# Spreading feed-forward filler and weight rounding over the turns of an attention loop

## The chip, the core and the metric

The kernel runs on one core of a Trainium2 chip. The metric is the device time of one execution in microseconds (us). Engines are named as in the profile: PE is TensorE, with PEld its weight loads; DVE is VectorE, ACT ScalarE, POOL GpSimd, SP the queue that issues most transfers.

## The reference

Cluster-routed attention, followed by a feed-forward network with a quick GELU. There are 4 batches, 8 heads, 768 positions and 64 dimensions a head; 3072 tokens of 512 features, and 2048 hidden features.

```python
q_assign = argmax(q_n @ c_n)           # nearest of 16 centroids, per head
k_assign = argmax(k_n @ c_n)
mask   = q_assign[..., :, None] == k_assign[..., None, :]
scores = where(mask, scale * q @ k.T, -1e9)
attn   = softmax(scores)
x = (attn @ v) -> (3072, 512)          # heads side by side
h = x @ w_in                           # w_in: 512 x 2048
out = (h * sigmoid(1.702 * h)) @ w_out # w_out: 2048 x 512
```

The weights come as 64-bit floats, and the kernel rounds them to 32 bits itself.

## The kernel before

The program has an attention loop of 96 turns and, after it, the feed-forward part of batches 1 to 3 (with seven products in place of eight for the first matrix). The feed-forward part of batch 0, two halves of 384 tokens, is cut into chunks and laid between the turns of the attention loop as filler for the PE. A turn handles two units (`u`); a unit is 128 keys of a head pair against 384 queries. Three turns make a group `g`, and 24 turns (`TB`) a batch.

A weight chunk (128 x 512) is rounded in two parts, a split and, one round later, a join:

```python
def split_w(i):
    nc.vector.tensor_scalar(out=e, in0=hi, scalar1=EXP, ...)             # DVE
    nc.vector.tensor_scalar(out=w.bitcast(I32), in0=hi, ...)             # DVE
    nc.scalar.activation(out=e, in_=e, func=AF.Relu, scale=8.0, ...)     # ACT
    nc.scalar.activation(out=w, in_=w.bitcast(I32), func=AF.Copy, ...)   # ACT

def join_w(i):
    nc.vector.scalar_tensor_tensor(out=e, in0=raw[:, :, 1], ..., in1=e)  # DVE
    nc.vector.scalar_tensor_tensor(out=w, in0=raw..[:, :, 0], ..., in1=w)
    nc.vector.tensor_tensor(out=w, in0=w, in1=e.bitcast(FP32), op=ALU.mult)

def round_next():          # one round: load i + 2, split i, join i - 1
    i = w_done[0]
    if i < NW:             # NW = 32 chunks: 16 of w_in, 16 of w_out
        load_w(i + 2)
        split_w(i)
    if 0 < i <= NW:
        join_w(i - 1)
    w_done[0] += 1
```

The filler, and what it ends with; `xT` holds features x 384 tokens:

```python
def normalise(g):                  # after each group
    ...                            # sums of the group by two products on the PE
    nc.vector.reciprocal(out=rec, in_=ps[:, 0:HALF])
    nc.vector.tensor_tensor(out=x, in0=x, in1=rec, op=ALU.mult)
    if g % HP == HP - 1 and g < 2 * HP:       # g = 3 and g = 7
        ffn.extend(ffn_chunks(g // HP))

def check(g):                      # ACT: two activations that read the reciprocals
    ...

def gelu(g, t, h):
    nc.scalar.activation(out=t, in_=h, func=AF.Tanh, scale=0.851)
    nc.vector.scalar_tensor_tensor(out=g, in0=t, scalar=1.0, in1=h,
                                   op0=ALU.add, op1=ALU.mult)

def ffn_chunks(bh):                # one half: 24 chunks, tile by tile of 128 tokens
    def first4(n, part):           # 16 products of 128 columns
        ps = bank()
        for i in range(4):
            f = 4 * part + i
            for c in range(NCH):
                nc.tensor.matmul(out=ps[:, i * P:(i + 1) * P],
                                 lhsT=w_in[:, c, f * P:(f + 1) * P],
                                 rhs=xT[c][:, n * P:(n + 1) * P], ...)
        g = gs[part] = gp.tile([P, 4 * P], FP32, name="g")
        gelu(g, g, ps)

    def second4(n, part):          # 4 products of 512 columns with w_out
        ...
    return [c for n in range(NH) for c in
            [((q + 1) * NCH, lambda n=n, q=q: first4(n, q)) for q in range(NF // 4)]
            + [(NW // 2 + 4 * (q + 1), lambda n=n, q=q: second4(n, q))
               for q in range(NF // 4)]]
```

The first number of a chunk is how many rounds it needs. The loop:

```python
for t in range(NT + 2):            # NT = 96
    ...                            # scores(u), part(u), exps(u) for the two units
    second_half = t >= TB // 2     # from turn 12 on
    if second_half and (t < TB or t % 2 == 0):
        round_next()
    ...                            # mask(u); values(u) of the turn before
    owed = owed + 0.6 if ffn else 0.0
    g = (t - 2) // TG if t >= 2 and (t - 2) % TG == TG - 1 else None
    if g is not None and second_half:
        normalise(g)
    ...                            # preparation of a later head pair
    if g is not None and not second_half:
        normalise(g)
    if recs:
        check(*recs)
    if not second_half:
        round_next()
    while (owed >= 1 and ffn and ffn[0][0] < w_done[0]
           and (t < TB + TB // 2 or len(ffn) > NF // 4)):
        ffn.popleft()[1]()
        owed -= 1
    if second_half and t < TB and t % 2:
        round_next()
```

So a turn does one round up to turn 11, one and a half on average from 12 to 23, and one every second turn after that, until the 33 are done at turn 28. In batch 0 (turns 0 to 23) the mask is part of the PE's scores; from turn 24 on it is four DVE operations a turn, each comparing cluster numbers and multiplying. Scores of a turn go to PSUM buffers (`ps_s`, 2) that the masks of the turn before set free. The last four chunks are left for after the loop, where the DVE makes sums of weights and inputs for the seven products.

Of the kernel before, what the change touches and what calls it, by code (L numbers as in the profile page):

```python
# [8 lines left out]
FP32 = mybir.dt.float32  # L9
# [29 lines left out]
def fast(  # L39
# [25 lines left out]
    nc = tc.nc  # L65
# [4 lines left out]
    P = 128  # L70
    NJ = S // P
    HALF = S // 2
    NH = NJ // 2
    HP = H // 2
    NPAIR = B * HP
    NCH = DM // P
    NF = DF // P
# [9 lines left out]
    xp = ctx.enter_context(tc.tile_pool(name="xp", bufs=NX))  # L87
    gp = ctx.enter_context(tc.tile_pool(name="gp", bufs=NF // 4))
# [13 lines left out]
        name="dram", bufs=2, space=bass.MemoryType.DRAM))  # L102
# [3 lines left out]
    def bank():  # L106
        return ps_m.tile([P, 512], FP32, name="m")

    def short():
        return tmp.tile([P, HALF], FP32, name="short")  # L110
# [28 lines left out]
    w_in = const.tile([P, NCH, DF], FP32, name="w_in")  # L139
    w_out = const.tile([P, NF, DM], FP32, name="w_out")  # L140
    WN = 512
# [6 lines left out]
    NW = len(w_chunks)  # L148
# [39 lines left out]
    w_done = [0]  # L188

    def round_next():  # L190
        i = w_done[0]
        if i < NW:
# [5 lines that stand above are left out]
# [50 lines left out]
    for a in range(2):  # L248
        rows = slice(a * D, (a + 1) * D)
        nc.vector.tensor_copy(  # L250
            out=cT[rows, :, a, :],
            in_=cps[rows, 0:P].rearrange("d (h a c) -> d h a c", a=2,
                                         c=NC)[:, :, a, :])
# [121 lines left out]
    s_of, A_of, sum_of, o_of, O_of, xT_of = {}, {}, {}, {}, {}, {}  # L375
# [6 lines left out]
    def scores(u):  # L382
        g, kt = divmod(u, NJ)
        p, h = split(g)
        ps = ps_s.tile([P, 2, 512], FP32, name="s")
        for a in range(2):
            rows = slice(a * D, (a + 1) * D)
            nc.tensor.matmul(out=ps[:, a, 0:HALF],  # L388
                             lhsT=T[p, 1][rows, kt * P:(kt + 1) * P],
                             rhs=T[p, 0][rows, h * HALF:(h + 1) * HALF],  # L390
                             start=True, stop=(p >= HP))
        s_of[u] = ps[:, :, 0:HALF]

    def part(u):

        g, kt = divmod(u, NJ)
        p, h = split(g)
        if p >= HP:
            return
        for a in range(2):  # L400
            r = 32 * (2 * (p % 2) + a)
            nc.tensor.matmul(
                out=s_of[u][:, a, :],
                lhsT=hots[p // 2, 1][r:r + NC, kt * P:(kt + 1) * P],
                rhs=hots[p // 2, 0][r:r + NC, h * HALF:(h + 1) * HALF],
                start=False, stop=True)

    def exps(u):
        p, h = split(u // NJ)
        s = s_of[u]  # L410
        if p < HP:
            A_of[u] = ap.tile([P, 2, HALF], FP32, name="A")
        nc.scalar.activation(out=A_of[u] if p < HP else s, in_=s, func=AF.Exp,  # L413
                             scale=SCALE)
# [23 lines left out]
    def values(u):  # L438
        g, kt = divmod(u, NJ)
        p, h = split(g)  # L440
        if kt == 0:
            o_of[g] = ps_o.tile([P, 512], FP32, name="o")
        A = A_of.pop(u)
        for a in range(2):
            nc.tensor.matmul(out=o_of[g][a * D:(a + 1) * D, 0:HALF],  # L445
                             lhsT=v_in[p][:, a, kt, :], rhs=A[:, a, :],
                             start=(kt == 0), stop=(kt == NJ - 1))
        if kt == NJ - 1:
            O_of[g] = xp.tile([P, HALF], FP32, name="x")
            nc.scalar.copy(O_of[g], o_of.pop(g)[:, 0:HALF])  # L450

    def normalise(g):

        sm = sum_of.pop(g)
        ps = bank()
        for a in range(2):
            nc.tensor.matmul(out=ps[a * D:(a + 1) * D, 0:HALF], lhsT=ones,  # L457
                             rhs=sm[:, a, :], start=True, stop=True)
        rec = recs[g] = short()
        nc.vector.reciprocal(out=rec, in_=ps[:, 0:HALF])  # L460
        x = xT_of[g] = O_of.pop(g)
        nc.vector.tensor_tensor(out=x, in0=x, in1=rec, op=ALU.mult)
        if g % HP == HP - 1 and g < 2 * HP:
            ffn.extend(ffn_chunks(g // HP))

    recs = {}

# [11 lines left out]
# [6 lines that stand above are left out]
    def second(bh, n, part, g, ps):  # L485

        for f in range(4 * part, 4 * part + 4):
            nc.tensor.matmul(out=ps[:, 0:DM], lhsT=g(f), rhs=w_out[:, f, :],  # L488
                             start=(f == 0), stop=(f == NF - 1))
        if part == NF // 4 - 1:  # L490
            b, h = divmod(bh, 2)
            y = yp.tile([P, DM], FP32, name="y")
            nc.scalar.mul(y, ps[:, 0:DM], 0.5)  # L493
            nc.sync.dma_start(
                out=out[b * S:(b + 1) * S, :].rearrange(
                    "(p j) n -> p j n", j=NJ)[:, h * NH + n, :], in_=y)
# [2 lines left out]

    ffn = deque()  # L500

    def ffn_chunks(bh):
        xT = [xT_of.pop(bh * HP + c) for c in range(NCH)]
        gs, ys = {}, {}

        def first4(n, part):
# [6 lines that stand above are left out]
                                     rhs=xT[c][:, n * P:(n + 1) * P],  # L513
                                     start=(c == 0), stop=(c == NCH - 1))
            g = gs[part] = gp.tile([P, 4 * P], FP32, name="g")
            gelu(g, g, ps)

        def second4(n, part):
            if part == 0:
                ys[n] = bank()  # L520
            g = gs.pop(part)
            second(bh, n, part,
                   lambda f: g[:, f % 4 * P:(f % 4 + 1) * P], ys[n])

        return [c for n in range(NH) for c in
                [((q + 1) * NCH, lambda n=n, q=q: first4(n, q))
                 for q in range(NF // 4)]
                + [(NW // 2 + 4 * (q + 1), lambda n=n, q=q: second4(n, q))
                   for q in range(NF // 4)]]


# [4 lines left out]
    TB = 2 * HP * TG  # L536

    prep_at = {}
    for p in range(1, NPAIR):
        b, hp = divmod(p, HP)  # L540
        for i in range(2 if p == 1 else 0, len(PREP)):
            if p == 1:
                t = (i - 2) // 2
            elif b == 0:
                t = (hp - 2) * TG + 1 + i // 2
            else:
                t = b * TB + (-8, -5, -2, 1)[hp] + i
# [5 lines left out]
    def prep(p, i):  # L553
        if i == 0 and p:
            load_v(p)
        PREP[i](p)
        if i in (1, 3) and loads:
            load_qk(*loads.popleft())

    owed = 0.0  # L560
# [4 lines left out]
    for t in range(NT + 2):  # L565
        us = range(2 * t, 2 * t + 2) if t < NT else ()
        for u in us:
            scores(u)
        if t == 0:
            prep(0, 6)  # L570
        for u in us:
            part(u)
        for u in us:
            exps(u)
        second_half = t >= TB // 2
        if second_half and (t < TB or t % 2 == 0):
            round_next()
        for u in us:
            mask(u)
        work = sorted(prep_at.get(t, ()), key=lambda w: PREP[w[1]] != prep_near)  # L580
        while work and PREP[work[0][1]] == prep_near:
            prep(*work.pop(0))
        if 1 <= t <= NT:
            for u in range(2 * t - 2, 2 * t):
                values(u)
        owed = owed + 0.6 if ffn else 0.0
        g = (t - 2) // TG if t >= 2 and (t - 2) % TG == TG - 1 else None
        if g is not None and second_half:
            normalise(g)
        for p, i in work:  # L590
            prep(p, i)
        if g is not None and not second_half:
            normalise(g)
        if recs:
            check(*recs)
        if not second_half:
            round_next()

        while (owed >= 1 and ffn and ffn[0][0] < w_done[0]
               and (t < TB + TB // 2 or len(ffn) > NF // 4)):  # L600
            ffn.popleft()[1]()
            owed -= 1
        if second_half and t < TB and t % 2:
            round_next()
    qcode.clear()
    att.close()
# [89 lines left out]
    XT = sums_x(1)  # L696
    sums_w(2 * P, FB * P)
    while ffn:
        ffn.popleft()[1]()

    ok = const.tile([P, 2, 2 * NPAIR], FP32, name="ok")
    nc.vector.tensor_scalar(out=ok, in0=sums, scalar1=LIMIT, scalar2=None,
# [5 lines left out]
    for b in range(1, B):  # L708
        gs = {}
        for f in range(FB):  # L710
            seven(f, *XT, gs)
        if b == B - 1:
            ps = bank()
# [5 lines left out]
        for h in range(2):  # L719
            for n in range(NH):  # L720
# [5 lines left out]
                ps = bank()  # L726
# [443 lines left out]
```

## Time and profile before

| | |
|---|---|
| time, median of 3 runs | 1110.47 us (1110.04 to 1111.21) |
| span of the profiled execution | 1107.3 us |
| PE busy | 1032.3 us, 93% |
| DVE busy | 608.0 us, 55% |
| ACT busy | 356.4 us, 32% |
| POOL busy | 297.0 us, 27% |
| mean granted TensorE clock | 0.976 |

The page gives busy times as shares of the span and as digits per slice, a fortieth of the span each. The costliest groups of instructions on the PE belong to the second matrix after the loop (L488, 247.7 us), the scores (L388, 161.8 us) and the values (L445, 150.7 us). On the DVE they are the masks (L424, 157.7 us), the sums of the seven products (L673, 93.3 us), and the reciprocals (L460, 81.6 us, 2551 ns each). An answer by windows gives the busy time of each engine in a stretch of time, a timeline the instructions in order; "[4.18 <-DVE A L424]" at a line's end is the idle time of its engine before it and the instruction that ended it. A busy PE is not a PE at its peak.

### The profile page before, as it was taken

How to read it: one execution, taken by the hardware profiler on the slowest of the kernel's cores; microseconds unless marked ns; L12 is line 12 of the kernel's file. 1: busy time of each engine (PE TensorE's matmuls, PEld its weight loads, DVE VectorE, ACT ScalarE, POOL GpSimd, SP SyncE). 2: the span in 40 equal slices, each digit the busy share in tenths (PEclk: the TensorE clock that was granted, in tenths of full speed). 3: DMA queues.
4: the chain of work that ended last, by engine and by line, in shares of the span. 5: the costliest groups of instructions: out<-in, count | busy, mean ns of one | idle time of the engine just before them, and what ended most of it. 6: DMA issues, size and time to landing. Idle time of an engine off the chain costs nothing. (4 is left out here: it accounts for less than half of the span.)

```text
span 1107.3 us, 11572 instructions
## 1 busy us (share of the span) xinstructions
PE 1032.3 (93%) x4398; PEld 523.3 (47%) x4398; DVE 608.0 (55%) x896; ACT 356.4 (32%) x633; POOL 297.0 (27%) x168
## 2 busy tenths in 40 slices
PE   7776887999999999999996899999999999999997
PEld 4322453364464453464462355544555444555443
DVE  3899988976576756666655776600166300465000
ACT  4655555444454444554434222100022000122000
POOL 2555332445544455444545200000000000000000
PEclk9998988999999999999997999999999999999999
DMA  7523444200122101220000000000000000000000
GB/s 215 149 80 98 135 125 145 65 24 1 38 71 73 39 1 28 54 72 8 18 1 1 0 11 1 0 20 19 20 0 1 10 19 20 9 1 1 20 20 21
DMA packets 64817, 45.20 MB, mean 41 GB/s; under 512 B 51952, under 2 KB 57584, under 8 KB 64752
## 3 DMA queue, kind: packets, MB, share of 16 engines
q1 hardware_dynamic: 64608, 44.33, 13.8%
q8 instruction: 37, 0.61, 0.2%
q14 instruction: 28, 0.23, 0.1%
q10 hardware_dynamic: 144, 0.03, 0.0%
HBM read 38.04 MB, written 6.31 MB: 40 GB/s over the span
## 5 line engine op out<-in xcount | busy, mean ns | idle before, releaser
L434 POOL TENSOR_TENSOR sum<-sum,A 128x768 f32<-128x768 f32 x128 | 236.4, 1847 | 255.9 <-DVE A L424 169.5
L488 PE MATMUL m<-w_out,gb 128*128 128x512 f32 x576 | 247.7, 592 | 0.0
L424 DVE SCALAR_TENSOR_TENSOR A<-qb,code,s 128x384 f32<-128x384 uint8 x288 | 157.7, 608 | 103.8 <-ACT s L413 81.7
L673 DVE TENSOR_TENSOR gb<-b,gb 128x384 f32<-128x384 f32 x168 | 93.3, 556 | 213.9 <-PE b L668 207.2
L388 PE MATMUL s<-T,T 64*128 64x384 f32 x768 | 161.8, 534 | 36.4 <-ACT A L413 21.7
L488 PEld LDWEIGHTS m<-w_out,gb 128*128 128x128 f32 x576 | 109.4, 190 | 137.1 <-issue 136.6
L445 PE MATMUL o<-A,inv 128*64 128x384 f32 x768 | 150.7, 513 | 5.7 <-DVE A L424 3.6
L413 ACT ACTIVATE s<-s 128x768 f32<-128x768 f32 x144 | 109.3, 789 | 58.4 <-PE s L388 58.1
L388 PEld LDWEIGHTS s<-T,T 64*128 64x128 f32 x768 | 67.5, 193 | 109.8 <-issue 33.4
L511 PE MATMUL m<-x,w_in 128*128 128x128 f32 x768 | 93.3, 281 | 5.1 <-ACT T L271 5.1
L511 PEld LDWEIGHTS m<-x,w_in 128*128 128x128 f32 x768 | 89.7, 196 | 12.5 <-issue 6.6
L481 ACT ACTIVATE th<-gb 128x768 f32<-128x768 f32 x48 | 40.4, 842 | 170.0 <-DVE gb L673 139.8
L493 ACT ACTIVATE y<-m 128x512 f32<-128x512 f32 x24 | 14.3, 595 | 247.0 <-PE m L488 233.9
L445 PEld LDWEIGHTS o<-A,inv 128*64 128x64 f32 x768 | 48.3, 139 | 94.0 <-issue 84.3
L488 PE MATMUL m<-w_out,g 128*128 128x512 f32 x192 | 88.9, 609 | 0.2 <-ACT T L271 0.2
L460 DVE RECIPROCAL short<-m 128x384 f32<-128x384 f32 x32 | 81.6, 2551 | 5.8 <-PE m L457 5.7
L434 POOL TENSOR_TENSOR sum<-A 128x768 f32<-128x768 f32 x32 | 59.3, 1854 | 67.5 <-DVE A L424 30.6
L668 PE MATMUL b<-T,w_in 128*128 128x384 f32 x192 | 69.8, 486 | 0.0
L668 PE MATMUL b<-x,S 128*128 128x384 f32 x192 | 69.8, 486 | 0.0
L668 PE MATMUL b<-x,w_in 128*128 128x384 f32 x192 | 66.3, 486 | 0.0
L482 DVE SCALAR_TENSOR_TENSOR gb<-th,gb 128x768 f32<-128x768 f32 x48 | 45.7, 953 | 21.8 <-ACT th L481 21.8
L488 PEld LDWEIGHTS m<-w_out,g 128*128 128x128 f32 x192 | 35.6, 194 | 41.9 <-issue 41.4
(89 smaller groups left out, 776.0 us busy)
## 6 DMA issues: line engine op xcount, KB each, us to landing
raw<-in_moe_w_in_dram SPq DMA_DIRECT2D x16, 512.0 KB, 4.6
raw<-in_moe_w_out_dram SPq DMA_DIRECT2D x16, 512.0 KB, 3.4
in<-in_q_dram SPq DMA_DIRECT2D x32, 192.0 KB, 3.9
in<-in_k_dram SPq DMA_DIRECT2D x32, 192.0 KB, 3.0
inv<-in_v_dram SPq DMA_DIRECT2D x16, 384.0 KB, 4.7
out_dram<-y SPq DMA_DIRECT2D x24, 256.0 KB, 2.0
qb<-line SPq DMA_DIRECT2D x12, 192.0 KB, 3.0
line<-row SPq DMA_DIRECT2D x12, 1.5 KB
```

What stands on the lines that cost most here:

```text
L388: nc.tensor.matmul(out=ps[:, a, 0:HALF], lhsT=T[p, 1][rows, kt * P:(kt + 1) * P], rhs=T[p, 0][rows, h * HALF:(h + 1) * HALF], start=True, ...
L413: nc.scalar.activation(out=A_of[u] if p < HP else s, in_=s, func=AF.Exp, scale=SCALE)
L424: nc.vector.scalar_tensor_tensor(out=A_of[u][:, a, :], in0=qcode[p][:, a, h * HALF:(h + 1) * HALF], scalar=code[p][:, kt % NH, 1, kt // NH ...
L434: nc.gpsimd.tensor_tensor(out=sum_of[g], in0=A_of[u - 1] if kt == 1 else sum_of[g], in1=A, op=ALU.add)
L445: nc.tensor.matmul(out=o_of[g][a * D:(a + 1) * D, 0:HALF], lhsT=v_in[p][:, a, kt, :], rhs=A[:, a, :], start=(kt == 0), stop=(kt == NJ - 1))
L460: nc.vector.reciprocal(out=rec, in_=ps[:, 0:HALF])
L481: nc.scalar.activation(out=t, in_=h, func=AF.Tanh, scale=0.851)
L482: nc.vector.scalar_tensor_tensor(out=g, in0=t, scalar=1.0, in1=h, op0=ALU.add, op1=ALU.mult)
L488: nc.tensor.matmul(out=ps[:, 0:DM], lhsT=g(f), rhs=w_out[:, f, :], start=(f == 0), stop=(f == NF - 1))
L511: nc.tensor.matmul(out=ps[:, i * P:(i + 1) * P], lhsT=w_in[:, c, f * P:(f + 1) * P], rhs=xT[c][:, n * P:(n + 1) * P], start=(c == 0), stop ...
L668: nc.tensor.matmul(out=ps[:, 0:HALF], lhsT=a(c), rhs=x(c), start=(c == 0), stop=(c == 1))
L673: nc.vector.tensor_tensor(out=o, in0=a, in1=b, op=ALU.add)
```

## The change

Three things change together.

- The first half of batch 0 no longer goes tile by tile. Its first matrix is done in 16 chunks of four products with 384 columns (`ffn_half`, `first`), each as soon as its part of w_in is rounded; the 16 results stay in buffers (12 of pool `x`, 4 of pool `g`), and 12 chunks of the second matrix follow. The second half (`ffn_tiles`) stays as it was.
- Every chunk has a cost and a rate: each turn earns the rate of the chunk that is next (2.4 for the first half, 1.6 for the second), up to 6.0, and a chunk is laid when its cost (2.6, 3.4 or 3.5) is earned. This is to spread the filler evenly over turns 15 to 91; before, chunks ran from 15 to 87.
- The rounds are stretched: two of three turns up to turn 11, one a turn from 12 to 23 with a second at every fourth, then three of four turns until turn 36.

```diff
         if g % HP == HP - 1 and g < 2 * HP:
-            ffn.extend(ffn_chunks(g // HP))
+            ffn.extend((ffn_half, ffn_tiles)[g // HP]())
...
+    def ffn_half():
+        xT = [xT_of.pop(c) for c in range(NCH)]
+        gs, ys = {}, {}
+        def first(f):
+            ps = bank()
+            for c in range(NCH):
+                nc.tensor.matmul(out=ps[:, 0:HALF],
+                                 lhsT=w_in[:, c, f * P:(f + 1) * P],
+                                 rhs=xT[c], start=(c == 0),
+                                 stop=(c == NCH - 1))
+            g = gs[f] = (xp.tile([P, HALF], FP32, name="x") if f % 4 else
+                         gp.tile([P, 4 * P], FP32, name="g")[:, 0:HALF])
+            gelu(g, g, ps[:, 0:HALF])
+        def second3(n, part):
+            if part == 0:
+                ys[n] = bank()
+            second(0, n, part, ..., ys[n])
+        return ([((f * P // WN + 1) * NCH, 2.6, 2.4, lambda f=f: first(f))
+                 for f in range(NF)]
+                + [(NW // 2 + 4 * (q + 1), 3.4, 2.4,
+                    lambda n=n, q=q: second3(n, q))
+                   for n in range(NH) for q in range(NF // 4)])
...
-                [((q + 1) * NCH, lambda n=n, q=q: first4(n, q))
+                [(NW, 3.5, 1.6, lambda n=n, q=q: first4(n, q))
                  for q in range(NF // 4)]
-                + [(NW // 2 + 4 * (q + 1), lambda n=n, q=q: second4(n, q))
+                + [(NW, 3.4, 1.6, lambda n=n, q=q: second4(n, q))
                    for q in range(NF // 4)]]
...
-        if second_half and (t < TB or t % 2 == 0):
+        if second_half and t < TB:
             round_next()
...
-        owed = owed + 0.6 if ffn else 0.0
+        owed = min(owed + ffn[0][2],
+                   6.0) if ffn else 0.0
...
-        if not second_half:
+        if t < TB // 2 and t % 3 < 2 or t >= TB and t % 4 < 3:
             round_next()
-        while (owed >= 1 and ffn and ffn[0][0] < w_done[0]
+        while (ffn and owed >= ffn[0][1] and ffn[0][0] < w_done[0]
                and (t < TB + TB // 2 or len(ffn) > NF // 4)):
-            ffn.popleft()[1]()
-            owed -= 1
-        if second_half and t < TB and t % 2:
+            owed -= ffn[0][1]
+            ffn.popleft()[3]()
+        if second_half and t < TB and t % 4 == 3:
             round_next()
```

More of the change, by code (lines that the diff above doesn't have):

```diff
@@ L500, in fast, with ffn_tiles @@
     ffn = deque()
-    def ffn_chunks(bh):
-        xT = [xT_of.pop(bh * HP + c) for c in range(NCH)]
+    def ffn_half():
[14 more added lines that the diff above has]
+                ys[n] = bank()
+            second(0, n, part,
+                   lambda f: (gs.pop(f) if n == NH - 1 else gs[f])[
+                       :, n * P:(n + 1) * P], ys[n])
+        return ([((f * P // WN + 1) * NCH, 2.6, 2.4, lambda f=f: first(f))
[3 more added lines that the diff above has]
+                   for n in range(NH) for q in range(NF // 4)])
+    def ffn_tiles():
+        xT = [xT_of.pop(HP + c) for c in range(NCH)]
         gs, ys = {}, {}
@@ L521, in second4 @@
             g = gs.pop(part)
-            second(bh, n, part,
+            second(1, n, part,
                    lambda f: g[:, f % 4 * P:(f % 4 + 1) * P], ys[n])
         return [c for n in range(NH) for c in
-                [((q + 1) * NCH, lambda n=n, q=q: first4(n, q))
+                [(NW, 3.5, 1.6, lambda n=n, q=q: first4(n, q))
                  for q in range(NF // 4)]
-                + [(NW // 2 + 4 * (q + 1), lambda n=n, q=q: second4(n, q))
+                + [(NW, 3.4, 1.6, lambda n=n, q=q: second4(n, q))
                    for q in range(NF // 4)]]
@@ L698, in fast @@
     while ffn:
-        ffn.popleft()[1]()
+        ffn.popleft()[3]()
     ok = const.tile([P, 2, 2 * NPAIR], FP32, name="ok")
```

## The prediction

> **What bounds the kernel now.** I read the slices of the page first, then busy time by stage, then the timeline of the worst stage. The page's slices (40, of 27.7 us each; digits are tenths of busy time, PEclk tenths of the granted TensorE clock):
>
> ```profile
> PE   7776887999999999999996899999999999999997
> ...
> DVE  3899988976576756666655776600166300465000
> ...
> PEclk9998988999999999999997999999999999999999
> ```
>
> The PE row is not full in slices 0 to 6 and in 21 and 22, and the clock falls in the same places. In slices 1 to 6 VectorE (DVE) stands at 8 to 9. From slice 23 on (637 us) the PE is full with work that the change leaves alone, so everything is decided before it.
>
> A turn of the attention loop issues eight score matmuls (L388 in the records; each fp32 matmul is two records). Counting them in the PE timeline gives the start of every turn: turn 0 at 12.75, turn 6 at 49.90, turn 12 at 84.60, 15 at 106.38, 24 at 187.42, 37 at 266.40, 89 at 578.82; the last sums end at 623.53. Busy time per engine in these stages (columns: stretch and length, PE, PEld, DVE, ACT, POOL, clock, DMA share, GB/s):
>
> ```profile
> core 0: us, PE busy (x) PEld busy (x) DVE busy (x) ACT busy (x) POOL busy (x), PEclk, DMA share, GB/s
> 12.75:49.90 37.15, 29.55 (x206) 14.07 (x205) 26.25 (x42) 22.27 (x41) 14.56 (x8) 1.00 0.59 163
> 49.90:84.60 34.70, 25.66 (x151) 9.38 (x151) 33.98 (x41) 21.14 (x39) 20.44 (x10) 0.95 0.34 103
> 84.60:106.38 21.78, 12.52 (x64) 4.36 (x64) 21.43 (x23) 10.74 (x20) 10.48 (x5) 0.84 0.31 95
> 106.38:187.42 81.04, 65.43 (x379) 36.36 (x379) 71.98 (x87) 42.12 (x78) 30.84 (x16) 0.85 0.44 133
> 187.42:266.40 78.98, 76.73 (x431) 39.99 (x431) 61.63 (x94) 37.84 (x71) 38.39 (x22) 1.00 0.17 44
> 266.40:578.82 312.42, 305.51 (x1729) 159.62 (x1729) 201.27 (x300) 140.05 (x258) 155.98 (x87) 1.00 0.14 36
> 578.82:623.53 44.71, 31.50 (x135) 11.83 (x133) 25.53 (x35) 15.75 (x29) 24.92 (x14) 0.81 0.00 1
> ```
>
> Turns 6 to 14 are VectorE's: 33.98 of 34.70 and 21.43 of 21.78 us. Turns 15 to 23 are mostly VectorE's. Turns 24 to 88 are the PE's (idle 2.3 and 6.9 us). Turns 89 to 95 are bound by neither: the filler is used up. What they wait for stands in the timeline:
>
> ```profile
> 594.91 1.58 PE L388 MATMUL s<-T,T 64*128 64x384 f32 x8
> ...
> 595.35 2.55 DVE L460 RECIPROCAL short<-m 128x384 f32<-128x384 f32 x1
> ...
> 598.67 0.52 ACT L472 ACTIVATE short<-short 128x384 f32<-128x384 f32 x1 [4.83 <-DVE x L462]
> ...
> 602.11 1.65 PE L388 MATMUL s<-T,T 64*128 64x384 f32 x4 [4.18 <-DVE A L424]
> ```
>
> Once in three turns (t = 1 modulo 3) a group is normalised. ScalarE's check of the reciprocal sits ahead of the next exponentials, so those, the masks and the scores after them come late, and the PE stands 4.18 us unless filler lies in between. A chunk at the end of turn 1 or 2 modulo 3 fills that gap; one at 0 modulo 3 does not. Around turn 62, with one chunk, only 0.55 us of it is left.
>
> **What the Trainium skill says.** "Perfetto Trace Analysis", Optimization Strategy, says that a kernel with regimes of different limits can gain from interleaving them. That is the case here: VectorE binds before 187 us and the PE after. The same page, Matmuls, says larger matmuls are more efficient. The trace agrees, a little: a tile chunk of 16 products of 128 columns runs from 311.26 to 314.93 (3.67 us for 2048 columns), while four records of 384 columns advance by 1.29 us:
>
> ```profile
> 637.30 1.45 PE L668 MATMUL b<-x,w_in 128*128 128x384 f32 x4
> 638.59 1.45 PE L668 MATMUL b<-T,S 128*128 128x384 f32 x4
> ```
>
> "TensorE: Matmul & The Clock Gate", Part 1 (The HAM clock gate), says the clock halves after an idle window of some 3.4 us. The trace agrees: after a 4.17 us gap the eight score matmuls at 586.01 took 2.93 us, against 1.56 at 591.33. So filled gaps also give back clock. "SBUF — State Buffer", SBUF: two separate sides, says that VectorE operations with two SBUF inputs and GpSimd operations that read SBUF lock each other out on a shared port. Rounding is full of the former; the trace shows a dearer round where GpSimd works (below), but doesn't prove that cause.
>
> **The change part by part.** Counts follow from the loop's conditions and from the order of the instructions on the PE.
>
> Costs. A round (two splits, three joins on VectorE) is the sum of five group means, 4.37 us for w_in and 3.99 for w_out; in turns 15 to 23 its lines took 62.0 us for 14 rounds, 4.43 each. Neighbours overlap in the records by about 0.06 us, so I count 4.1, and 3.7 for w_out later. Chunks on the PE: tile chunk f 3.67 us; second product s or S 8 records of 0.43 (247.7 us / 576), 3.5 with its edges; new F (384 columns, four products) 2 x 1.29 = 2.58. Gelu on VectorE: 0.69 for f, about 0.55 for F (L673's 384 columns took 0.556), 0.63 and 0.5 without overlap.
>
> Rounds per stage, before to after: turns 0-11 12 to 8; 12-14 4 to 3; 15-23 14 to 12; 24-36 3 to 10. Chunks: 15-23 4f+1s to 9F; 24-36 4f+4s to 7F+3S; from 37 on 16f+15s to 12f+17s. The last four s stay behind the loop in both.
>
> 1. Turns 0-11 (71.85 us): four rounds less take about 16 from VectorE's 60.2, leaving 44; the PE has 55.2, some 2 of it from slow clock. Both leave room, so latencies and startup show: I take 33 for turns 0-5 and 29 for 6-11, a gain of 10.
> 2. Turns 12-14 (21.78): VectorE 21.4 - 4.1 = 17.3; still the bound. Gain 4.5.
> 3. Turns 15-23 (81.04): VectorE 72.0 - 2 x 4.1 + 9 x 0.5 - 4 x 0.63 = 65.8. PE: 65.4 less about 8 (clock 0.85) plus 23.2 - 18.2 = 62.4. Two nearly equal loads that wait for each other; 72 us, a gain of 9.
> 4. Turns 24-36 (78.98): VectorE 61.6 - 10.5 (the old rounding lines in this stretch) + 37 + 1 = 89, above the PE's 76.7, which hardly changes (28.6 against 28.7 of chunks). At the 96% density of the old VectorE stretches: 93 to 94, a loss of 15. The bottleneck moves here and takes back most of steps 1 and 2.
> 5. Turn 37 to the end of the loop (357.1): PE busy 337.0, of which about 7 is slow clock (seven bare turns at 1.49 + 1.44, three sums at 0.8 and the last values come to 24.4 us warm, not 31.5). Chunks: 111.2 to 103.5. That leaves 322.5 of PE work. Idle: groups with one well placed chunk 10 x 0.6, those with two 6 x 0.2, turns 61-63 (sole chunk at 63, wrong place) 4.2, turns 94 on, without filler, 5, and 1.5 of clock: 18. So 340.5, a gain of 16.5.
>
> Sum: -10 - 4.5 - 9 + 15 - 16.5 = -25, so 1110.5 - 25 = 1085 us.
>
> **The rivals.** (a) VectorE in turns 24 to 36 gets worse than dense: each F's gelu waits in order behind a round, and the exponentials sit behind ScalarE's part of the round. Then step 4 costs 25 and the kernel stands near 1095 or higher, "same". For it: ScalarE's rounding work does sit ahead of the exponentials. Against it: in turns 6 to 14, with the same order, VectorE was 98% busy. (b) The early turns don't get shorter: the matmul, copy and exponential latencies bind and not VectorE. Then steps 1 to 3 bring 10, and the result is about 1098. For it: turns 0-5 have VectorE at 26 of 37 us. Against it: turns 6-14 at 98%. (c) Early stages run at the larger of the two loads and the clock stays full, and VectorE's overload at 24-36 is partly absorbed: steps 1 to 3 bring 30, step 4 costs 10, step 5 brings 20: about 1070. (d) The even filling is worth nothing because idle latency merely moves: then step 5 yields only the 7.7 us of moved chunks, total near 1094.
>
> **Range and chances.** The errors of five stages, about 4 us each, partly common, give some 9 to 10 us; 8 in 10 is 1068 to 1101. The 2% line is 1088.3, only 3 us above my value, so faster by over 2% gets 0.58, within 2% 0.39. Slower by 2% would need step 4 at twice its size and nothing elsewhere: 0.03.
>
> **What would show it.** Right: turn 24 starts near 164 us instead of 187; turns 24-36 take about 94 us with VectorE above 90% busy and the PE near 80%; the gaps of 4.2 us after 578 us are gone but for one near turn 95 and one near turn 63; the loop ends near 598. Wrong: turn 24 after 175 us (rival b); turns 24-36 beyond 100 us (a) or under 88 (c); gaps of 3 us and more before the scores in most late groups in spite of a chunk (d).

## The result, and the profile after

The changed kernel takes 1099.28 us, the median of 4 runs (1098.40 to 1100.98), against 1110.56 us before: a ratio of 0.9900, with a 95% interval of 0.9883 to 0.9917. That is 11.3 us less, where 25 were predicted. The time lies inside the predicted range, close to its upper end.

The slices of the page after (40, now of 27.5 us):

```profile
PE   7888879988999998999999899999999999999997
...
DVE  3479998999656764677667766500266300465000
...
PEclk9988999999999999999999899999999999999999
```

The PE row still has gaps in its first ten slices; the dip of slices 21 and 22, 6 and 8 before, is down to a single 8. The stages, cut at the same turns as before (0, 12, 15, 24, 37, 89 and the last sums); columns as in the prediction's table:

```profile
11.03:84.86 73.83, 59.56 (x356) 25.46 (x355) 44.25 (x69) 40.63 (x74) 33.27 (x18) 0.88 0.42 115
84.86:100.42 15.56, 13.52 (x64) 4.95 (x64) 14.54 (x16) 8.46 (x16) 10.21 (x5) 0.82 0.30 96
100.42:177.59 77.17, 67.15 (x314) 30.35 (x315) 68.81 (x75) 41.10 (x79) 34.48 (x17) 0.96 0.42 122
177.59:270.66 93.07, 81.32 (x351) 35.24 (x351) 86.53 (x132) 44.95 (x85) 37.59 (x21) 0.96 0.25 72
270.66:573.31 302.65, 292.46 (x1555) 141.07 (x1553) 201.09 (x297) 136.97 (x253) 157.01 (x88) 0.99 0.14 38
573.31:614.55 41.24, 35.27 (x199) 17.24 (x197) 26.40 (x37) 17.02 (x31) 24.70 (x14) 0.94 0.00 1
```

VectorE (third column after the length) lost the 16 us of busy time in turns 0 to 11 that step 1 took off it, 60.2 to 44.3, and the stage became no shorter: 71.85 to 73.83 us. This is the heart of the matter. The program was profiled a second time; its first row there:

```profile
11.43:81.81 70.38, 55.75 (x356) 23.99 (x356) 44.28 (x69) 40.55 (x74) 33.67 (x18) 0.95 0.42 119
```

The same instructions, the same VectorE time, and 3.5 us less, with a granted clock of 0.95 in place of 0.88. So some 3 us of an early stage is how the clock's slow windows fall, and differences of that size there are not to be explained. Two experiments below repeat these turns unaltered: the first has the kernel before's instructions in them and took 74.03 us (clock 0.90), the second has the change's and took 70.38 (0.95). So, by these four executions, the change made this stage at most 3.7 us shorter. The stages side by side:

| turns | before | predicted | after | after, second profile |
|---|---|---|---|---|
| 0 to 11 | 71.85 | 62 | 73.83 | 70.38 |
| 12 to 14 | 21.78 | 17.3 | 15.56 | 15.71 |
| 15 to 23 | 81.04 | 72 | 77.17 | 77.21 |
| 24 to 36 | 78.98 | 94 | 93.07 | 93.26 |
| 37 to the last sums | 357.1 | 340.5 | 343.9 | 343.8 |
| the four chunks left over | 13.8 | 13.8 | 14.6 | 14.6 |

Of the gain that is missing, 8 to 12 us are in turns 0 to 11, 5 in turns 15 to 23 and 3 from turn 37 on; turns 12 to 14 gave nearly 2 us more than predicted.

### The profile page after: what moved, and what is told of

It is laid out like the page before. It is cut to its first block, busy times and chain, and to the rows that moved or that the text cites. A ratio compares the mean times of both kernels' runs of the same rounds, so it can differ in the third digit from the quotient of the medians.

```text
span 1099.2 us, 11063 instructions
## 1 busy us (share of the span) xinstructions
PE 1034.0 (94%) x4142; PEld 501.7 (46%) x4142; DVE 607.1 (55%) x900; ACT 355.3 (32%) x637; POOL 298.6 (27%) x168
## 5 line engine op out<-in xcount | busy, mean ns | idle before, releaser
L424 DVE SCALAR_TENSOR_TENSOR A<-qb,code,s 128x384 f32<-128x384 uint8 x288 | 157.7, 609 | 96.2 <-ACT s L413 84.2
L388 PE MATMUL s<-T,T 64*128 64x384 f32 x768 | 163.6, 535 | 29.1 <-DVE A L424 15.3
L413 ACT ACTIVATE s<-s 128x768 f32<-128x768 f32 x144 | 109.4, 787 | 55.7 <-PE s L388 55.0
L388 PEld LDWEIGHTS s<-T,T 64*128 64x128 f32 x768 | 67.8, 193 | 110.0 <-issue 37.2
L488 PE MATMUL m<-w_out,g 128*128 128x512 f32 x120 | 57.2, 611 | 0.0
L472 ACT ACTIVATE short<-short 128x384 f32<-128x384 f32 x32 | 16.7, 523 | 123.4 <-DVE x L462 123.4
L511 PE MATMUL m<-x,w_in 128*128 128x384 f32 x128 | 47.7, 519 | 6.7 <-DVE x L482 3.2
L700 PEld LDWEIGHTS b<-x,w_in 128*128 128x128 f32 x192 | 36.5, 190 | 26.1 <-issue 1.4
```

What stands on the lines that cost most here:

```text
L388: nc.tensor.matmul(out=ps[:, a, 0:HALF], lhsT=T[p, 1][rows, kt * P:(kt + 1) * P], rhs=T[p, 0][rows, h * HALF:(h + 1) * HALF], start=True, ...
L424: nc.vector.scalar_tensor_tensor(out=A_of[u][:, a, :], in0=qcode[p][:, a, h * HALF:(h + 1) * HALF], scalar=code[p][:, kt % NH, 1, kt // NH ...
L511: nc.tensor.matmul(out=ps[:, 0:HALF], lhsT=w_in[:, c, f * P:(f + 1) * P], rhs=xT[c], start=(c == 0), stop=(c == NCH - 1))
L700: nc.tensor.matmul(out=ps[:, 0:HALF], lhsT=a(c), rhs=x(c), start=(c == 0), stop=(c == 1))
```

## The experiments

Two accounts were set against each other. In theory A the early turns hang on a chain: sums on the PE, reciprocal on VectorE, check on ScalarE, and only then the next exponentials. In theory B they hang on VectorE's load, as the prediction had it. (Experiment 4 has a pair of its own, and the later ones narrow theory A down.) Each timed run is compared with the kernel before on the same chip (1109.8 to 1110.4 us).

### 1 and 2. Each half of the change alone

The filler with the old rounding:

```diff
-        if second_half and t < TB:
+        if second_half and (t < TB or t % 2 == 0):
...
-        if t < TB // 2 and t % 3 < 2 or t >= TB and t % 4 < 3:
+        if not second_half:
             round_next()
...
-        if second_half and t < TB and t % 4 == 3:
+        if second_half and t < TB and t % 2:
```

> The change's filler with the old rounding (all rounds done by turn 28). Theory A (the stretched rounding is worth nothing net: turns 0 to 14 hang on the chain of normalising, not on VectorE's load, and turns 24 to 36 pay for the moved rounds): turns 24 to 36 back at 80 to 83 us, turns 0 to 23 some 8 to 14 us longer than in the change, the late turns 37 to the end as short as in the change (about 344 us), in all 1097 to 1101 us, like the change. Theory B (stretching brings a part of the gain): 1103 to 1107 us.

Measured: 1105.81 us, ratio 0.9958 (0.9943 to 0.9972). The filler alone brings 4.6 us; theory A's total failed, and B's was right; A's 80 to 83 us for turns 24 to 36 failed too. The late turns are as short as in the change (303.06 + 41.25 = 344.3 us). Turns 24 to 36:

```profile
189.33:274.85 85.52, 79.90 (x352) 34.89 (x351) 61.70 (x100) 37.92 (x72) 36.52 (x21) 0.96 0.15 37
```

Here VectorE has its old load, 61.7 us, and the stage is still 6.5 us longer than before: PE busy 3.2 us more, idle 3.4 us more, clock 0.96 instead of 1.00. So of the 14 us lost there in the change, 6.5 came with the filler and 7.5 with the moved rounds.

The stretched rounding with the old filler puts the change's three round conditions into the kernel before:

```diff
-        if second_half and (t < TB or t % 2 == 0):
+        if second_half and t < TB:
...
-        if not second_half:
+        if t < TB // 2 and t % 3 < 2 or t >= TB and t % 4 < 3:
...
-        if second_half and t < TB and t % 2:
+        if second_half and t < TB and t % 4 == 3:
```

> The old filler (chunks by tile, 0.6 a turn) with the stretched rounding. Theory A: the late turns keep their empty tail, turns 0 to 36 gain and lose about the same, 1107 to 1113 us, like the kernel before. Theory B: 1102 to 1106 us.

Measured: 1135.64 us, ratio 1.0234 (1.0211 to 1.0257). Both theories missed this. The old filler keeps strict order and has no cap on what is owed, so its seventh and eighth chunks waited for late w_out chunks until turns 30 and 36, and six came in turn 36 alone, which took 27.4 us; turns 24 to 36 took 121 us. Stretching alone is a loss; it pays only together with a filler that starts on w_in and needs w_out late. From 1105.8 to 1099.3 it brings 6.5 us.

### 3. The skipped round in the normalising turn

```diff
-        if t < TB // 2 and t % 3 < 2 or t >= TB and t % 4 < 3:
+        if t < TB // 2 and t % 3 != 1 or t >= TB and t % 4 < 3:
```

> The change, but up to turn 11 the turn without a round is the one that normalises (t = 1 modulo 3) in place of the one after it (t = 2); 8 rounds as before. Theory A (the round's ScalarE part, 0.72 + 0.62 us, and its first VectorE operations sit between the check and the exponentials): the gaps of 2.4 to 4.1 us before the scores of turns 5, 8 and 11 shrink by 1.3 to 2 us each, turns 0 to 11 by 3 to 6 us, in all about 1095 us. Theory B (VectorE's load): the same number of rounds, so no difference, 1098 to 1101 us.

Measured: 1097.80 us, ratio 0.9884 (0.9867 to 0.9900), whose interval overlaps with that of the change; the profile tells more. The idle time of the PE before the scores of a turn (the gaps stand before turns 6, 9, 12 and 15; the expectation's 5, 8 and 11 are the turns whose exponentials are late):

| PE idle before turn | 6 | 9 | 12 | 15 |
|---|---|---|---|---|
| before | 2.37 | 4.14 | 3.99 | 7.45 |
| change | 2.36 | 4.14 | 3.17 | 2.04 |
| this run | 0.29 | 3.01 | 2.05 | 8.06 |

Three gaps shrink by 1.1 to 2.1 us, with as many rounds as in the change. The four rounds that the change leaves out at t = 2 modulo 3 had stood beside the chain; those in it were kept. The chain ahead of turn 9 in the kernel before: the check (L472), the round's two ScalarE operations (L171, L173), the exponentials (L413), the scores (L388):

```profile
64.75 0.52 ACT L472 ACTIVATE short<-short 128x384 f32<-128x384 f32 x1 [2.78 <-DVE x L462]
...
66.01 0.70 ACT L171 ACTIVATE e<-e,low 128x512 int32<-128x512 int32 x1
66.62 0.61 ACT L173 ACTIVATE w_in<-w_in 128x512 f32<-128x512 int32 x1
67.26 1.51 ACT L413 ACTIVATE A<-s 128x768 f32<-128x768 f32 x2
...
68.12 2.38 PE L388 MATMUL s<-T,T 64*128 64x384 f32 x8 [4.14 <-ACT A L413]
```

The same in the change:

```profile
65.16 0.52 ACT L472 ACTIVATE short<-short 128x384 f32<-128x384 f32 x1 [2.77 <-DVE x L462]
...
66.42 0.70 ACT L171 ACTIVATE e<-e,low 128x512 int32<-128x512 int32 x1
67.04 0.61 ACT L173 ACTIVATE w_in<-w_in 128x512 f32<-128x512 int32 x1
67.67 1.51 ACT L413 ACTIVATE A<-s 128x768 f32<-128x768 f32 x2
...
68.54 2.93 PE L388 MATMUL s<-T,T 64*128 64x384 f32 x8 [4.14 <-ACT A L413]
```

In this run no round stands between the check (here ahead of turn 12) and the exponentials:

```profile
76.43 0.52 ACT L472 ACTIVATE short<-short 128x384 f32<-128x384 f32 x1 [3.94 <-DVE x L462]
...
77.69 1.49 ACT L413 ACTIVATE A<-s 128x768 f32<-128x768 f32 x2
...
78.53 1.61 PE L388 MATMUL s<-T,T 64*128 64x384 f32 x8 [2.05 <-ACT A L413]
```

Turns 0 to 11 are shorter, with more VectorE time (46.67 us) than in the change:

```profile
11.87:78.53 66.66, 57.30 (x356) 24.57 (x355) 46.67 (x67) 39.18 (x72) 33.06 (x18) 0.92 0.44 124
```

The gap before turn 15 takes most of it back:

```profile
85.07 2.30 DVE L182 SCALAR_TENSOR_TENSOR w_in<-raw,w_in 128x512 f32<-128x512 uint32 x1
...
87.41 2.18 DVE L185 TENSOR_TENSOR w_in<-w_in,e 128x512 f32<-128x512 f32 x1
...
92.23 2.55 DVE L460 RECIPROCAL short<-m 128x384 f32<-128x384 f32 x1
...
97.58 2.93 PE L388 MATMUL s<-T,T 64*128 64x384 f32 x8 [8.06 <-ACT A L413]
```

The rounds of turns 11 to 13 now follow one another ahead of turn 13's reciprocal.

### 4. Four of five GpSimd additions left out

```diff
-        if kt == 0:
+        if kt < NJ - 1:
             return
-        if kt == 1:
+        if True:
             sum_of[g] = ap.tile([P, 2, HALF], FP32, name="sum", bufs=2)
         nc.gpsimd.tensor_tensor(out=sum_of[g],
-                                in0=A_of[u - 1] if kt == 1 else sum_of[g],
+                                in0=A_of[u - 1],
```

The sum of a group holds only its last two units, so this kernel leaves out most of the softmax's denominator.

> Leaves out four of the five GpSimd additions of a group (the sum is that of the last two units only); the rest as in the change. Theory A (the rounding's VectorE operations are long only while a GpSimd addition holds the shared port): the five operations of a round fall to 0.42, 0.42, 0.68, 0.68 and 0.69 us nearly everywhere, 2.9 us a round; VectorE's busy time in turns 24 to 36 falls from 86.5 to about 77 us, and in turns 0 to 11 from 44 to about 38, while the length of turns 0 to 11 changes by under 3 us. Theory B (a round's cost is VectorE's own): the durations stay between 0.42 and 2.3 us with the same means.

Measured: 1066.88 us in one run. In turns 15 to 23 the rounding's 55 VectorE operations fall from 55.2 to 37.0 us, and the stage becomes the PE's alone:

```profile
93.19:156.40 63.21, 62.92 (x314) 28.96 (x314) 49.54 (x75) 41.48 (x79) 8.07 (x4) 1.00 0.52 148
```

It was 77.17 us with VectorE at 68.81. Turns 24 to 36: 93.07 to 86.86 us, VectorE 86.5 to 80.0. Turns 0 to 11: 68.4 us, against 70.4 and 73.8. The durations didn't fall to their least everywhere, since one addition in five is left and still meets some rounds, and the direction is A's; the sizes are smaller, 6.5 us of VectorE time in turns 24 to 36 where 9.5 were expected, and 2.2 in turns 0 to 11 where 6 were. GpSimd's sums themselves also take less time in this run, so it isn't shown that all of the 14 us in turns 15 to 23 come by way of VectorE's operations. What GpSimd costs a round is seen in the change's own timeline, VectorE first:

```profile
66.32 0.68 DVE L182 SCALAR_TENSOR_TENSOR w_in<-raw,w_in 128x512 f32<-128x512 uint32 x1
67.04 0.69 DVE L185 TENSOR_TENSOR w_in<-w_in,e 128x512 f32<-128x512 f32 x1
...
69.05 2.29 DVE L182 SCALAR_TENSOR_TENSOR w_in<-raw,w_in 128x512 f32<-128x512 uint32 x1
71.37 2.18 DVE L185 TENSOR_TENSOR w_in<-w_in,e 128x512 f32<-128x512 f32 x1
```

and GpSimd in the same stretch:

```profile
62.90 1.81 POOL L434 TENSOR_TENSOR sum<-sum,A 128x768 f32<-128x768 f32 x1
68.63 4.38 POOL L434 TENSOR_TENSOR sum<-sum,A 128x768 f32<-128x768 f32 x2 [3.91 <-ACT A L413]
73.59 1.81 POOL L434 TENSOR_TENSOR sum<-A 128x768 f32<-128x768 f32 x1 [0.59 <-ACT A L413]
```

The same two operations take 0.68 and 0.69 us while GpSimd is idle and 2.29 and 2.18 us while it adds. The trace books the difference as VectorE's busy time. A round alone is 0.42 + 0.42 + 0.68 + 0.68 + 0.69 = 2.9 us; the 4.1 of the prediction is a mean over both kinds. In the trace before, 22 of 32 operations of L167, the first of a split, meet no addition and take 0.41 to 0.43 us; the ten that do average 1.62.

### 5. No rounds at all up to turn 11

```diff
-        if t < TB // 2 and t % 3 < 2 or t >= TB and t % 4 < 3:
+        if t >= TB and t % 4 < 3:
             round_next()
...
-        if second_half and t < TB and t % 4 == 3:
+        if second_half and t < TB:
             round_next()
```

> The change without any round up to turn 11; turns 12 to 23 do two each instead (24 in all by turn 24 instead of 23). Read for the length of turns 0 to 11 alone. Theory A (those turns consist of PE work, the chain over reciprocal, check and exponentials, and slow clock; VectorE's rounds were never their bound): 65 to 71 us, that is at most 5 us less than the 70.4 and 73.8 us measured with eight rounds. Theory B (the prediction's: VectorE's load binds, 4.1 us a round): 56 to 61 us. Turns 12 to 23 will be longer, in all 1102 to 1125 us.

Measured: 1115.92 us in one run. Turns 0 to 11:

```profile
11.77:72.67 60.90, 53.70 (x357) 23.54 (x356) 23.10 (x34) 31.61 (x58) 32.55 (x18) 0.97 0.31 83
```

60.9 us is under theory A's 65 to 71 and inside B's 56 to 61: by the length alone this run speaks for B, and A as I had put it is wrong, for the rounds do delay these turns. But the length doesn't follow VectorE's load. The eight rounds took 21.2 us off VectorE (44.28 to 23.10) and 9.5 off the second profile of the change; the four rounds fewer of the change had taken 16 us off VectorE and next to nothing off the stage; experiment 3 had more VectorE time and was shorter; and experiment 11, below, has the late check, eight rounds and 47.7 us of VectorE time, and takes 62.3 us, only 1.4 us longer than this run with none. What a round costs depends on where it lies. Turns 15 to 23 pay with 94.2 us.

### 6. The check one turn later

```diff
         for u in us:
             exps(u)
+        if recs:
+            check(*recs)
...
             normalise(g)
-        if recs:
-            check(*recs)
...
+    if recs:
+        check(*recs)
     qcode.clear()
```

Nothing is left out; ScalarE's two checking activations come behind the next exponentials instead of ahead of them.

> The change, with ScalarE's two checking activations issued one turn later, behind the next turn's exponentials; nothing is left out. Theory A (the stall once in three turns comes from the check: ScalarE waits for the reciprocal before it may start the next exponentials): the 4.2 us gap before the scores of turn 63 falls below 1.5 us, turns 0 to 11 come to 66 to 70 us, turn 24 starts 6 to 12 us earlier, in all 1082 to 1091 us. Theory B (the stall comes from VectorE's order, masks and rounds behind the reciprocal, whatever ScalarE does): the gaps stay above 3 us and the time at 1097 to 1101 us.

Measured: 1075.12 us, ratio 0.9683 (0.9666 to 0.9699), better than theory A's range. Turn 63 in the change, where the one chunk near it lies in the wrong place:

```profile
421.22 2.55 DVE L460 RECIPROCAL short<-m 128x384 f32<-128x384 f32 x1
...
423.80 0.71 DVE L462 TENSOR_TENSOR x<-x,short 128x384 f32<-128x384 f32 x1
424.55 0.52 ACT L472 ACTIVATE short<-short 128x384 f32<-128x384 f32 x1 [4.83 <-DVE x L462]
...
425.81 1.48 ACT L413 ACTIVATE s<-s 128x768 f32<-128x768 f32 x2
...
427.98 2.70 PE L388 MATMUL s<-T,T 64*128 64x384 f32 x8 [4.18 <-DVE A L424]
```

and with the late check:

```profile
407.25 2.55 DVE L460 RECIPROCAL short<-m 128x384 f32<-128x384 f32 x1
407.82 1.50 ACT L413 ACTIVATE s<-s 128x768 f32<-128x768 f32 x2 [2.08 <-PE s L388]
...
409.84 0.70 DVE L462 TENSOR_TENSOR x<-x,short 128x384 f32<-128x384 f32 x1
410.46 2.18 DVE L424 SCALAR_TENSOR_TENSOR A<-qb,code,s 128x384 f32<-128x384 uint8 x4
410.58 0.52 ACT L472 ACTIVATE short<-short 128x384 f32<-128x384 f32 x1 [1.25 <-DVE x L462]
...
411.74 1.97 PE L388 MATMUL s<-T,T 64*128 64x384 f32 x8 [1.90 <-DVE A L424]
```

The exponentials go before the reciprocal is ready; the gap falls to 1.90 us, not below the 1.5 I expected, since the masks (L424) still stand behind the reciprocal on VectorE. Turns 37 to the last sums fall from 343.9 to 331.3 us: the PE's busy time from 327.7 to 322.6, at a clock of 1.00, and its idle time from 16.2 to 8.7. Turns 12 to 14 fall from 15.6 to 12.4. In turns 0 to 11 the gaps before turns 6, 9 and 12 remain (1.46, 3.23, 3.83 us), so there the check was not the whole chain.

### 7 to 9. The late check in other company

The same edit in the kernel before:

> The kernel before, with the same late check. Theory A: the unfilled turns 89 to the end fall from 44.7 to 32 to 36 us and the kernel to 1088 to 1098 us, so that most of what the even filler brought late (13 us) is had without it. Theory B: 1108 to 1112 us.

Measured: 1095.15 us, ratio 0.9860 (0.9844 to 0.9876); the unfilled turns 89 to the end take 36.8 us. Turns 37 to the last sums take 344.7 us here and 343.9 in the change, but the even filler and the late check are not two cures for one stall: from 357.1 they bring 12.4 and 13.2 us apart, and 25.8 together. The late check cuts the PE's idle time there (20.1 to 11.1 us); the change cuts its busy time above all (337.0 to 327.7, part of it chunks moved to earlier turns) and its idle time less (20.1 to 16.2). In all the change brings 20.0 us on top of the late check (1095.15 to 1075.12), more than without it; 9.5 of them are in turns 12 to 14 (21.9 to 12.4 us).

The late check, and no round in a normalising turn, up to turn 11 and from turn 24 (`t >= TB and t % 3 != 1`):

> The late check, and no round in a turn that normalises (t = 1 modulo 3), up to turn 11 and from turn 24 to 38. Theory A with a second part of the chain in the round's ScalarE operations, which wait behind the reciprocal: 2 to 6 us less than the late check alone. If that part doesn't matter once the check is gone: within 1.5 us of it.

Measured: 1086.37 us, 11 us slower than the late check alone; neither expectation. Turns 0 to 11 gained 6 us (62.3), but the rounds now end at turn 38, a chunk of the second matrix waited 4.5 us for its last weights, and the filler came late: turns 37 to 48 took 85.5 us against 78.1. Two edits in one run; experiment 11 keeps only the first.

The late check with the old rounding and the new filler:

> The late check with the change's filler and the old rounding. If the stretched rounding helps because fewer rounds meet GpSimd's additions and the reciprocals in turns 0 to 23 (load and lock): 4 to 8 us slower than the late check alone, as it was without it (6.5 us). If it helped only by leaving ScalarE's chain free: within 2 us.

Measured: 1084.69 us, 9.6 us slower than the late check with the stretched rounding, outside both expectations but on the side of the first. So what stretching brings is not only room in ScalarE's chain; with the check gone from it, stretching helps no less. Turns 12 to 14 take 21.9 us here against 12.4, turns 0 to 11 72.2 against 68.3.

### 10. The change once more

The unchanged program, for its profile.

> The change itself once more, for a second profile. If the slow clock of turns 0 to 11 (18.2 us of slow windows in the first profile, 7.5 in the same program up to turn 14 with the old filler) is a matter of how the clock's windows fall, it comes out differently here, between 3 and 15 us, and turns 0 to 11 at 68 to 73 us; if it belongs to the program, 18 us and 73.8 again.

Measured: 1098.29 us in one run, turns 0 to 11 at 70.38 us and a clock of 0.95, as shown above: it came out differently.

### 11. Both, early only

The late check, and `t % 3 != 1` up to turn 11 only.

> The late check, and up to turn 11 (only there) no round in the turn that normalises. Theory A: ScalarE's part of the round is the rest of the chain there; turns 0 to 11 come to 62 to 64 us, turns 12 to 14 pay 4 to 5 us back (a round just before the reciprocal of turn 13), in all 1071 to 1075 us against 1075.1. If it is paid back in full: 1075 to 1078 us.

Measured: 1073.18 us, median of 5 runs, ratio 0.9657 (0.9638 to 0.9676), the fastest version here; it beats both kernels, by 37 and 26 us. Its interval overlaps with that of the late check alone (0.9666 to 0.9699), so what the second edit adds isn't settled. All four gaps of the table above, before turns 6, 9, 12 and 15, are gone (0.00); turns 0 to 11 take 62.3 us, turns 12 to 14 17.7, and gaps of 2.69 and 2.98 us stand before the scores of turns 10 and 13, where the rounds of turns 9 and 12 are stretched beside additions (operations of 0.42 us take 2.03).

## Why the prediction missed

**Step 1 failed (turns 0 to 11, "a gain of 10"; the two profiles show 1.5 gained and 2.0 lost).** It took VectorE's load for what bounds these turns. VectorE lost the 16 us reckoned, yet turns 0 to 5 kept their 37.2 us ("33" in the prediction), and turns 6 to 11 went from 34.7 to 33.1 in the second profile ("29"). What bounds them is the chain over reciprocal, check, the round's ScalarE operations and exponentials: before turn 9 the PE stood 4.14 us in both kernels. "Turns 6 to 14 are VectorE's: 33.98 of 34.70" took busy time for work. Part of it was operations drawn out while GpSimd added, and the rounds that were left out lay beside the chain. The rounds in the chain stayed, and moving just those out closed 4.3 us of three gaps and made the stage 4 to 7 us shorter. That the 16 us came out exactly was luck: 23.1 us of VectorE time are left when no round is there, so twelve rounds took 37.1, or 3.1 each in place of 4.1, and the four that went happened to be the drawn-out ones, 4.0 each.

**Step 2 (turns 12 to 14, a gain of 4.5) was better than written:** 6.2 us. These turns did follow VectorE, but it lost 6.9 us there (21.43 to 14.54) where one round of 4.1 was reckoned.

**Step 3 (turns 15 to 23, a gain of 9) brought 3.9.** Its loads were right within a few us (VectorE 68.8 for 65.8; PE 67.15 at a clock of 0.96 for 62.4 at full, and 62.9 at full in experiment 4). The allowance for two equal loads that wait for each other was 6 us above the larger, and 8.4 was needed. With four fifths of GpSimd's additions gone the stage took 63.2 us, so most of the excess goes with the additions.

**Step 4 (turns 24 to 36, a loss of 15) was right in size, 14.1,** with two small misses that cancel: VectorE's load was 86.5 us in place of 89, and its share of the stage 93% in place of 96%. Its cause was half right: the filler alone costs 6.5 us there.

**Step 5 (turn 37 on, a gain of 16.5) brought 13.2.** The single gaps were right: 4.18 us before turn 63, and 0.18 and 0.67 before turns 90 and 93, which have a chunk near them. The PE was idle for 16.2 us (18 reckoned) and busy for 327.7 (322.5 reckoned). The same products took 322.6 us with the late check, at a clock of 1.00, so the work was right, and what the step had too little of is slow clock (it allowed 1.5 us). Of the 13.2 us, 9.3 are busy time and only 3.9 are idle time.

Rival (b) came nearest: the early turns hardly get shorter, steps 1 to 3 bring 10, the kernel lands near 1098. Turn 24 started at 187.42 us before, and starts at 177.59 in the first profile of the change and 174.73 in the second, on both sides of the 175 named as the rival's mark; so these steps with the start-up brought 9.8 and 12.7 us of 23.5. The rival is right for turns 0 to 11. It isn't for turns 12 to 14, which did get shorter, nor in its reason for turns 15 to 23. I had set it aside because VectorE was 98% busy; that was the very number that could not be trusted.

Of the places from the Trainium skill, the first was applied too widely: turns 0 to 11 were no regime of VectorE's. The others hold. "SBUF — State Buffer", SBUF: two separate sides, was cited as a doubt and turned out to bear on it: durations three to five times as long come when GpSimd adds, in single-input operations (0.42 to 2.0 us) and two-input operations (0.68 to 2.3 us), while the masks, which read PSUM, average 0.61 us with and without an addition beside them. That it is waiting for a shared port is the page's account; the runs show the coincidence and that it goes as the additions go.

Left open: how much of the difference between late check and late check with early edits is real, and whether GpSimd's additions and the rounds could be laid so that they don't meet. That wasn't tried.

## What to carry to other kernels

An engine at 98% is not the bound until its operations are shown to take their least time: compare the durations of one group with and without a neighbour engine at work before you subtract load. Where work is taken off an engine, ask whether the pieces removed lie in the chain that ends the other engine's gaps; equal gaps before and after say that they did not. And an instruction that merely keeps books, here a check, can hold up what its engine does after it: two such activations moved behind the exponentials took 24 us off the change.

## What the runs showed of the hardware

A VectorE operation of 0.42 us took up to 2.05 us, and one of 0.68 up to 2.3, while GpSimd worked through additions of 1.85 us, so a round of 2.9 us was seen to take over 10 us (turn 12 of the third experiment: 1.92 + 2.04 + 2.30 + 2.30 + 2.18). The same program had a granted clock of 0.88 and of 0.95 over its first twelve turns in two executions, 3.5 us apart there.
